# One MLP half step between the two parts of a head's first maximum, and the split of x behind the next head's roundings

## The chip, the cores and the metric

The kernel runs on one core of a Trainium2 chip. Its engines work side by side, each through its own instruction queue, in the order of that queue: TensorE (PE in the profile; its weight loads are PEld), VectorE (DVE), ScalarE (ACT), GpSimd (POOL) and SyncE (SP), which issues most of the DMAs. Where an instruction needs another engine's result, or a buffer that another engine still reads, it waits on a semaphore. The metric is the device time of one execution in microseconds (us), as the median of several runs. Every matmul writes a bank of PSUM; there are eight banks of 128 x 512 fp32, and ACT and DVE read them.

## The reference

Attention with a decay and a causal mask over 64 heads (8 batches of 8) of 576 positions and width 64, followed by an MLP without bias over all 4608 tokens.

```python
scores = scale * np.matmul(q, k.transpose(0, 1, 3, 2))
cum = np.cumsum(np.log(np.clip(f, 0.0001, 1.0)), axis=-1)
scores = np.where(causal, -1e9, scores + cum[:, :, :, None] - cum[:, :, None, :])
scores = scores - np.max(scores, axis=-1, keepdims=True)
attn = np.exp(scores)
attn = attn / (np.sum(attn, axis=-1, keepdims=True) + 1e-09)
x = np.matmul(attn, v)      # heads side by side: 4608 x 512
h = np.maximum(x @ w_in, 0.0)      # 512 -> 2048
out = h * h @ w_out      # 2048 -> 512
```

## The kernel before

**Slots.** The order of the program is written out by hand. A loop over slots n runs from before the first head to after the last. Head h has the six slots 6h to 6h+5, one for each unit u of its scores: a block of 128 keys against the queries that may see it (`UNITS`; the first one has 320 columns, the third 192). In slot n the loop (L810 on) emits, in this order: the split of the last slot's exponentials if it is still due (`split_last`), the score of unit u with its exponential (`score`), the products with V of the unit two slots back (`av_part`), steps that divide by the sums (`finish`), the events of the slot's first half, a share of the weight conversion (`cv`), MLP work (`fill(n, 0.5)`), the events of its second half, again `cv`, and `fill(n, 1.0)`. At the end `in_order` fixes that order on PE, ACT, DVE and POOL: no instruction passes another one of its engine.

**Maxima.** The maximum of each row of a head's scores is taken during the slots of the head before, in six units (`max_units`). A unit is a matmul of the rounded q (`r2`) by the rounded k (`kl0`) at L390, and a reduction by DVE at L398, which the profile shows as a custom operation and a read of the accumulator into the tile tcol. The first row block, that of the last 128 queries, has 576 columns, more than a bank holds. So it takes two units: maximum 0 with 256 columns, and maximum 1 with 320, whose reduction starts from the result of maximum 0. From head 10 on the events stand at `MAXIMA[1]`, slots 1.5, 2, 2.5, 3, 3.5 and 4 of the head before: maximum 0 in the second half of slot 6h+1, maximum 1 in the first half of slot 6h+2, maximum 2 in its second half. "Head 43's maximum 0" below means the one that is taken in head 43's slots (for head 44).

**Roundings.** `r2` and `kl0` are rounded copies of q and k. `prep` and, from head 20 on, `prep_split` make them on DVE (L335 and L336, or L357 and L358) in the second half of slot 6h, for the next head.

**MLP halves.** Chunks of 256 tokens (`T`), 16 steps each (`NF`). One step has two halves: `mlp1` (L605: 12 matmuls of 256 columns, x by w_in) and `mlp2` (L638: 6 matmuls of 512 columns, the squared relu by w_out), which belongs to the step before. `mlp_half` places them by turns. Each call first runs `bend` for the last `mlp1`, if that is still to come: ACT reads its bank for the relu (r, L620) and squares it (gh, L621), DVE makes the square and its low part (g, gl, L625 and L626). All `mlp1` write one bank, number 4 (`banks["h"]`), so each must wait until the relu of the one before has read it. With 12 and 6 matmuls per step and heads of 6 scores, one `mlp1` or `mlp2` stands between most groups of attention matmuls.

**Pace.** `fill` spreads a batch's halves evenly over the slots in which the next batch's attention runs. `ready[b]` is the slot from which the chunks that batch b completes are open: 53, 104, 152, 200, 248, 296, 344 and 392. Between two of them come 64 halves, or 96 (from slot 200 to 248, heads 33 to 41); `goal` is the count that is due at (n, part), and never above `limit`. After the loop, all that is left of the MLP follows in one run.

**Banks.** Scores and maxima share banks by turns (`banks["s"]`): four from the start of the MLP on, only two ([1, 2]) while chunk 1 is worked on (from head 10's last slot to head 17's slot 2), then four again.

**The split of x.** `split_x` makes of a chunk's x a rounded part xh (L590) and a low part xl (L591), both on DVE. It follows POOL's multiply of x by the reciprocals (`finish`, part 3, L537). For batches 1 to 7 it is an event of slot `ready[b] - 2`, that is slot 6h of head h = 17, 25, 33, 41, 49, 57 and 65 (the last behind the last head), in its first half; `finish` part 3 stands in the same slot, ahead of it.

Of the kernel before, what the change touches and what calls it, by code (L numbers as in the profile page):

```python
# [34 lines left out]
def decay_attention_relu2_kernel(  # L35
# [20 lines left out]
    NH, D, _, S = qk.shape  # L56
# [7 lines left out]
    T = 256  # L64
# [219 lines left out]
    NU = len(UNITS)  # L284
# [375 lines left out]
    def mlp_half(finished):  # L660
        bend()
        if halves[0] % 2:
            if len(steps) > 1:
                mlp2(*steps[-2])
        else:
            step = next_step()
            if step is None:
                return False
            c, fc = step
            if fc == 0:  # L670
                if c == 0:
                    banks.update(s=[1, 2, 3, 5], m=[], av=[0])
                if c == 1:
                    banks.update(s=[1, 2], o0=[3], o1=[5])
                if c == 2:
                    banks.update(s=[1, 2, 3, 5], o0=[6], o1=[7])
                split_x(c, finished)
            if fc > 0 and ("x", c + 1) not in mst and (c != 1 or ahead[0] == NF):
                split_x(c + 1, finished)
            mlp1(c, fc)  # L680
            ahead[c] += 1
            steps.append(step)
        halves[0] += 1
        return True
# [9 lines left out]
    MAXIMA = (0, 0.5, 1, 1.5, 2, 2.5), (1.5, 2, 2.5, 3, 3.5, 4)  # L694
# [7 lines left out]
    def split_last():  # L702
        while unsplit:
            split_p(*unsplit.pop())

    def fin(h, part):

        return (h + 1) * NU - 1 + DIVIDE[h >= H][part]
# [13 lines left out]
    ready = [fin(b * H + H - 1, 3) + 2 if b else H * NU + 5 for b in range(B)]  # L722

    def fill(n, part):

        b = sum(r <= n for r in ready)
        if b == 0:
            return
        r0 = ready[b - 1]
        r1 = ready[b] if b < B else r0 + H * NU  # L730
        limit, before = (2 * NF * (x * S // T) for x in (b, b - 1))
        goal = before + (limit - before) * (n - r0 + part) / (r1 - r0)
        if b == 1 and len(split_w) == NW:

            if not pace:
                pace.append((n + part, halves[0]))
            n0, h0 = pace[0]
            goal = h0 + (limit - h0) * (n + part - n0) / (r1 - n0)
        while halves[0] < min(goal, limit):
            split_last()  # L740
            if not mlp_half(b):
                break
# [11 lines left out]
    def at(n, half, do, *args):  # L754
        events.setdefault((n, half), []).append(lambda: do(*args))
# [22 lines left out]
        if not split:  # L778
            at((h - 1) * NU + (4 if h else 3), 0, turn_maxima, h)
    for b in range(B):  # L780
        at(ready[b] - (2 if b else 1), 0, split_x, b * S // T, b + 1)
    spun = psum.tile([P, 512], F32, name="bank6")

    def spin(n):
# [25 lines left out]
    for n in range(-2 * NU, last_slot + 1):  # L810
        live = 0 <= n < len(slots)
        split_last()
        if live:
            h, u = slots[n]
            score(h, u)
            if h >= NPLAIN:
                unsplit.append((h, u))
        for ha, ua in avs.get(n, ()):
            if ua < NU - 1:
                av_part(ha, ua, False)  # L820
            else:
                av_part(ha, ua, True)
                av_part(ha, ua - 1, True)
        for do, *args in fins.get(n, ()):
            do(*args)
        for do in events.get((n, 0), ()):
            do()
        wr = 0 if n < -NU // 2 else RATES[0 if n < 0 else 1 if n < ready[0] else 2]
        cv(wr / 2)
        fill(n, 0.5)  # L830
        for do in events.get((n, 1), ()):
            do()
        cv(wr / 2)
        fill(n, 1.0)
# [45 lines left out]
```

## Time and profile before

| what | us |
|---|---|
| median of 3 runs | 1202.7 (1198.0 to 1205.06) |
| the profiled execution's own time | 1200.4 |
| its span, first to last instruction | 1198.7 |

The mean clock granted to TensorE over the span is 0.995. The span has three parts: up to some 250 us, in which also the weights are converted and heads with other forms of the scores run; the heads from 18 to 63, about 16.2 us each (21.7 where a batch has 96 halves), up to some 1040 us; and the rest of the MLP alone. The work of each engine in one stretch of each part (us of the window, then busy us and, in brackets, instructions of PE, PEld, DVE, ACT and POOL; the granted clock; the share of time that DMA engines were busy, and GB/s):

```profile
100.00:200.00 100.00, 97.03 (x616) 80.46 (x614) 79.40 (x203) 64.11 (x158) 5.29 (x14) 1.00 0.45 119
700.00:800.00 100.00, 100.00 (x690) 91.93 (x689) 66.34 (x185) 63.37 (x165) 39.48 (x60) 1.00 0.20 48
1000.00:1100.00 100.00, 99.54 (x660) 90.53 (x659) 46.24 (x118) 44.35 (x114) 14.44 (x23) 1.00 0.08 22
```

A row of a timeline has the start in us from the span's begin, the duration in us, the engine, the line, the operation, output and inputs by the program's names, their shape, and a count. In square brackets stands how long the engine had been idle before it, and what released it. A matmul's row lasts longer than its share of PE, because matmuls overlap: the distance from one start to the next is what PE spends.

### The profile page before, as it was taken

To read this page: it belongs to the slowest core of one execution; us is meant where nothing else is said; L and a number is where in the kernel's file an instruction comes from. 1 tells how busy PE (TensorE), PEld (TensorE's weight loads), DVE (VectorE), ACT (ScalarE), POOL (GpSimd) and SP (SyncE) were. 2 spreads that over 40 slices of the span, in tenths; PEclk is the share of its full clock that TensorE was granted. 3 is DMA by queue.
4 is the path that set the end of the run, shared out by engine and by line. 5 is a ranking of instruction groups with operands and counts; after the bars stand their busy time and mean duration, and the time that the engine had idled before them with its cause. 6 is when DMAs were issued, how large, how long until landed. Compare 5 with 4: busy or idle time off the path is not lost. (4 is left out here: it accounts for less than half of the span.)

```text
span 1198.7 us, 23146 instructions
## 1 busy us (share of the span) xinstructions
PE 1174.7 (98%) x7770; PEld 1040.0 (87%) x7770; DVE 773.1 (64%) x2072; ACT 693.5 (58%) x1745; POOL 317.8 (27%) x510
## 2 busy tenths in 40 slices
PE   7999999999999999999999999999999999999998
PEld 4667887789998999899999899988999899999997
DVE  6888887666667666756666666676676766443232
ACT  4776666555666665665565656666665666533232
POOL 2110000123334343422222334344333434200000
PEclk8999999999999999999999999999999999999999
DMA  8885622221211121211111122112121112000000
GB/s 200 198 226 175 175 51 51 70 69 43 54 37 46 42 60 43 54 32 35 42 45 24 53 43 54 42 33 60 42 61 36 42 42 60 12 28 19 1 19 18
DMA packets 109778, 73.03 MB, mean 61 GB/s; under 512 B 90766, under 2 KB 90766, under 8 KB 109660
## 3 DMA queue, kind: packets, MB, share of 16 engines
q1 hardware_dynamic: 108936, 68.90, 22.6%
q0 software_dynamic: 720, 2.65, 1.0%
q8 instruction: 62, 1.02, 0.4%
q14 instruction: 56, 0.46, 0.1%
q10 hardware_dynamic: 4, 0.00, 0.0%
HBM read 58.41 MB, written 9.87 MB: 57 GB/s over the span
## 5 line engine op out<-in xcount | busy, mean ns | idle before, releaser
L638 PE MATMUL bank<-w,gh 128*128 128x512 f32 x1152 | 413.5, 399 | 0.0
L605 PE MATMUL bank<-xh,w 128*128 128x256 f32 x2304 | 331.5, 286 | 5.5 <-ACT r L620 5.4
L605 PEld LDWEIGHTS bank<-xh,w 128*128 128x128 f32 x2304 | 300.1, 189 | 16.9 <-ACT r L620 9.8
L470 DVE TENSOR_TENSOR pl<-p,ph 128x320 fp32r<-128x320 f32 (+4 forms) x288 | 175.4, 610 | 203.3 <-ACT ph L469 198.5
L638 PEld LDWEIGHTS bank<-w,gh 128*128 128x128 f32 x1152 | 217.5, 189 | 37.8
L638 PE MATMUL bank<-w,gl 128*128 128x512 f32 x576 | 227.0, 394 | 0.2 <-DVE gl L626 0.2
L469 ACT CAST ph<-p 128x320 fp32r<-128x320 f32 (+4 forms) x288 | 119.4, 415 | 162.8 <-POOL p L456 119.8
L456 POOL TENSOR_SCALAR_AFFINE_SELECT p<-p 128x128 f32<-128x128 f32 (+1 forms) x240 | 87.1, 363 | 392.1 <-ACT p L454 324.9
L620 ACT ACTIVATE r<-bank 128x256 f32<-128x256 f32 x288 | 109.7, 381 | 132.4 <-PE bank L605 118.3
L605 PE MATMUL bank<-xl,w 128*128 128x256 f32 x1152 | 184.6, 283 | 0.0
L454 ACT ACTIVATE p<-bank 128x320 f32<-128x320 f32 (+4 forms) x288 | 111.2, 386 | 117.9 <-PE bank L442 105.4
L625 DVE TENSOR_TENSOR g<-r 128x256 f32<-128x256 f32 x261 | 115.5, 443 | 94.3 <-ACT r L620 94.3
L626 DVE TENSOR_TENSOR gl<-g,gh 128x256 fp32r<-128x256 f32 x288 | 135.9, 472 | 47.9 <-ACT g L623 16.8
L398 DVE CUSTOM_DVE_ANT_0 bank<-bank,mz 128x256 f32<-128x256 f32 (+4 forms) x320 | 133.6, 432 | 49.7 <-PE bank L390 49.2
L605 PEld LDWEIGHTS bank<-xl,w 128*128 128x128 f32 x1152 | 158.4, 191 | 0.2 <-DVE xl L591 0.2
L621 ACT ACTIVATE gh<-r 128x256 fp32r<-128x256 f32 x288 | 120.4, 418 | 9.1
L390 PE MATMUL bank<-rk 66*128 66x320 f32 (+4 forms) x384 | 110.7, 318 | 12.3 <-DVE tcol L398 4.1
L638 PEld LDWEIGHTS bank<-w,gl 128*128 128x128 f32 x576 | 109.2, 190 | 15.1 <-DVE gl L626 1.7
L442 PE MATMUL bank<-rl 128*128 128x320 f32 x324 | 95.1, 294 | 0.0
L439 PE MATMUL bank<-rk 67*128 67x320 f32 x324 | 93.4, 288 | 0.1
L390 PEld LDWEIGHTS bank<-rk 66*128 66x128 f32 (+1 forms) x384 | 67.6, 182 | 28.7 <-DVE tcol L398 6.9
L480 PE MATMUL bank<-pl,vh 128*65 128x320 f32 (+4 forms) x336 | 91.3, 272 | 0.0
(103 smaller groups left out, 1485.3 us busy)
## 6 DMA issues: line engine op xcount, KB each, us to landing
qkraw<-in_qk SPq DMA_DIRECT2D x54, 288.0 KB
v<-in_v SPq DMA_DIRECT2D x64, 160.0 KB
out<-osb SPq DMA_DIRECT2D x36, 256.0 KB
den<-rdr SPq DMA_DIRECT2D x62, 144.0 KB
w<-in_w_in SPq DMA_DIRECT2D x16, 512.0 KB
w<-in_w_out SPq DMA_DIRECT2D x16, 512.0 KB
rk<-tcol SPq DMA_DIRECT2D x216, 0.5 KB
rl<-in_qk SPq DMA_DIRECT2D x10, 288.0 KB
```

What stands on the lines that cost most here:

```text
L390: nc.tensor.matmul(ps[:m, :n], st["r2"][:D + 2, q0:q0 + m], st["kl0"][:D + 2, k0:k0 + n], start=True, stop=True,)
L398: nc.vector.tensor_tensor_reduce(out=ps[:m, :n], in0=ps[:m, :n], in1=mz[:m, mo:mo + n], op0=ALU.add, op1=ALU.min, scale=-1.0, scalar=init, ...
L442: nc.tensor.matmul(ps[:kn, :n], st["l2"][:, k0:k0 + kn], st["r1"][:, q0:q1], start=False, stop=not added,)
L454: nc.scalar.activation(out=p[:kn, :n], in_=ps[:kn, :n], func=AF.Exp, scale=SCALE)
L469: nc.scalar.copy(out=ph[:kn, :n], in_=p[:kn, :n])
L470: nc.vector.tensor_tensor(out=pl[:kn, :n], in0=p[:kn, :n], in1=ph[:kn, :n].bitcast(F32), op=ALU.subtract,)
L605: nc.tensor.matmul(ph[:, :T], w[:, s, cc], x[:, cc, :], start=(cc == 0 and k == 0), stop=(cc == NCC - 1 and k == 2),)
L620: nc.scalar.activation(out=r, in_=ph[:, :T], func=AF.Relu)
L621: nc.scalar.activation(out=gh, in_=r, func=AF.Square)
L625: nc.vector.tensor_tensor(out=g, in0=r, in1=r, op=ALU.mult)
L626: nc.vector.tensor_tensor(out=gl, in0=g, in1=gh.bitcast(F32), op=ALU.subtract)
L638: nc.tensor.matmul(po, g[:, ts], w[:, s], start=(fc == 0 and k == 0), stop=(fc == NF - 1 and k == 2),)
```

## The change

Two edits; no instruction is added or left out, and only the order changes.

```diff
@@ fill(n, part)
             n0, h0 = pace[0]
             goal = h0 + (limit - h0) * (n + part - n0) / (r1 - n0)
+        if n % NU == int(MAXIMA[1][0]) and part == 1:
+            goal += 1
         while halves[0] < min(goal, limit):
             split_last()
             if not mlp_half(b):
@@
     for b in range(B):
-        at(ready[b] - (2 if b else 1), 0, split_x, b * S // T, b + 1)
+        at(ready[b] - (2 if b else 1), 1 if b else 0, split_x, b * S // T, b + 1)
```

The first edit raises the goal by one half step in the second `fill` of each slot 6h+1 (`int(1.5)` is 1), behind maximum 0 and ahead of the score of unit 2 and maximum 1. The goal of the next call is as it was, so the total doesn't change. It acts from slot 55 (head 9) on, and not where the goal has reached the batch's limit.

The second edit moves the split of x for batches 1 to 7 from the first half of slot `ready[b] - 2` to its second half. Events of one half run in the order in which they were entered, and those of the heads were entered first, so the split now comes after `prep` part 0 of the next head, which has the two roundings.

## The prediction

> **What bounds the kernel now.** I read the page first, then TensorE's waits, the chain that ended last, and the timelines around one head's first maximum.
>
> ```profile
> span 1198.7 us, 23146 instructions
> PE 1174.7 (98%) x7770; PEld 1040.0 (87%) x7770; DVE 773.1 (64%) x2072; ACT 693.5 (58%) x1745; POOL 317.8 (27%) x510
> L605 PE MATMUL bank<-xh,w 128*128 128x256 f32 x2304 | 331.5, 286 | 5.5 <-ACT r L620 5.4
> ```
>
> TensorE (PE) is busy for 98% of the span, and no other engine for more than 64%. So time is gained only where PE stands still, and each new stand of PE is lost unless it swallows an old one. The waits of PE alone (engine, line, what it waited for; us in total, times, longest):
>
> ```profile
> engine line waited for: us in total, times, longest us
> PE bank L605 <- ACT r L620: 5.4, 8, 0.8
> PE bank L390 <- DVE tcol L398: 4.1, 5, 1.0
> PE bank L390 <- DVE rk L358: 1.8, 3, 0.9
> PE bank L390 <- DVE rk L336: 0.8, 1, 0.8
> ```
>
> The change can win from two of these. Rows 2 to 4 are maxima (L390) that wait for a reduction on DVE (VectorE; tcol) or for the next head's roundings (rk): 6.7 us in all. Row 1 names the danger: the first product of an MLP step (mlp1, L605) waits for the relu (r, L620) on ACT (ScalarE), because all mlp1 share one PSUM bank, and the relu of the last mlp1 must have read it.
>
> **The change, first edit: where the half goes.** In `fill` the goal of a batch that does 64 halves in 48 slots is a whole number at the end of slot 6h+1, so there the kernel before places nothing. One more makes it place exactly one half, and the next call none. By parity that half is an mlp1. Per head PE's order was: mlp2, maximum 0, score of unit 2 with its value products, maximum 1, mlp1, maximum 2, mlp2. It becomes: mlp2, maximum 0, **mlp1**, score, value products, maximum 1, maximum 2, mlp2. The work is the same; mlp1 is only asked for earlier. ACT's order up to the relu doesn't change, since the relu is issued with the mlp2 ahead of maximum 0. Head 44, PE and ACT:
>
> ```profile
> 712.34 0.55 ACT L454 ACTIVATE p<-bank 128x448 f32<-128x448 f32 x1 [1.76 <-PE bank L442]
> ...
> 717.00 0.41 ACT L469 CAST ph<-p 128x256 fp32r<-128x256 f32 x1 [2.09 <-POOL rl L356]
> ...
> 722.13 0.38 ACT L620 ACTIVATE r<-bank 128x256 f32<-128x256 f32 x1
> ...
> 721.67 0.28 PE L390 MATMUL bank<-rk 66*128 66x256 f32 x1
> 721.79 0.25 PE L439 MATMUL bank<-rk 67*128 67x192 f32 x1
> ...
> 722.57 0.62 PE L605 MATMUL bank<-xh,w 128*128 128x256 f32 x3
> ```
>
> Maximum 0 starts at 721.67 and the score behind it at 721.79: there the moved mlp1 will stand. But the relu runs from 722.13 to 722.51, and mlp1 started 0.06 later, at 722.57. The old place had no slack at all. The new one asks 0.78 us sooner, so PE waits 722.57 − 721.79 = 0.78 us. The neighbour, head 43, has a little less:
>
> ```profile
> 705.71 0.25 PE L439 MATMUL bank<-rk 67*128 67x192 f32 x1
> ...
> 705.85 0.39 ACT L620 ACTIVATE r<-bank 128x256 f32<-128x256 f32 x1
> ...
> 706.49 1.11 PE L605 MATMUL bank<-xh,w 128*128 128x256 f32 x8
> ```
>
> Relu end 706.24, plus 0.06, less 705.71: 0.59 us. Here mlp1 started 0.25 us behind the relu, so it didn't wait before.
>
> Does the relu come earlier once PE stands? From 717.00 to the relu ACT has no idle time (none of its rows there shows any), on a run that begins behind POOL (GpSimd) and goes back to the exponential at 712.34, which waited 1.76 us for PE's score of unit 4. So it is with the exponentials at large:
>
> ```profile
> ACT p L454 <- PE bank L442: 105.4, 106, 1.8
> ```
>
> That score lies behind the new stand of the head before. So PE's delay moves the run along with it, and the stand comes back in each head.
>
> I read the same two times in each head concerned: 18 to 24, 26 to 32, 42 to 48, 50 to 56 and 58 to 63, 34 in all. (Heads 17, 25, 33, 41, 49 and 57 are at the batch's limit at that slot and get no extra half.) The first and the last:
>
> ```profile
> 252.36 0.38 ACT L620 ACTIVATE r<-bank 128x256 f32<-128x256 f32 x1
> 252.47 0.26 PE L439 MATMUL bank<-rk 67*128 67x192 f32 x1
> ...
> 1032.02 0.38 ACT L620 ACTIVATE r<-bank 128x256 f32<-128x256 f32 x1
> ...
> 1032.13 0.25 PE L439 MATMUL bank<-rk 67*128 67x192 f32 x1
> ```
>
> These two give 0.33 each, the others 0.52 to 0.86; the sum is **23.5 us**, a mean of 0.69.
>
> A stand also has a tail. Where PE waited for a relu, weights and matmul start together:
>
> ```profile
> 681.62 0.38 ACT L620 ACTIVATE r<-bank 128x256 f32<-128x256 f32 x1
> ...
> 682.05 1.01 PEld L605 LDWEIGHTS bank<-xh,w 128*128 128x128 f32 x8 [0.85 <-ACT r L620]
> 682.05 1.22 PE L605 MATMUL bank<-xh,w 128*128 128x256 f32 x8 [0.74 <-ACT r L620]
> ...
> 683.58 0.39 PE L638 MATMUL bank<-w,gh 128*128 128x512 f32 x1
> ...
> 1190.75 1.43 PE bank L605 x12
> ```
>
> From 682.05 to 683.58 is 1.53 us, against 1.43 for twelve undisturbed matmuls (the row of the chain): 0.10 for the weights that weren't loaded ahead. Heads like 44 pay this already, since their mlp1 starts on the relu's heels. I add it for the 16 that don't, like 43: 1.6 us. First term: 23.5 + 1.6 = **+25.1**. The Trainium skill ("TensorE: Matmul & The Clock Gate", the steps of what happens when a matmul is issued) says that PE pulls weight loads ahead of matmuls in flight, while matmuls keep their order. By that the 1.6 could go, and the 23.5 not; the load at 682.05, which waited with its matmul, doesn't agree for a load whose matmul is held, so I keep the 1.6.
>
> Heads 34 to 40 do 96 halves in 48 slots and have an mlp2 already between maximum 0 and the score; the moved mlp1 goes behind it (head 35):
>
> ```profile
> 540.16 0.40 PE L638 MATMUL bank<-w,gh 128*128 128x512 f32 x1
> ...
> 540.46 0.39 ACT L620 ACTIVATE r<-bank 128x256 f32<-128x256 f32 x1
> ...
> 541.56 0.25 PE L439 MATMUL bank<-rk 67*128 67x192 f32 x1
> ```
>
> The relu ends at 540.85, long before 541.56: no stand. Only in head 36 does it end about 0.1 us too late; with the tail 0.2 us. Without mlp2 as a cover, each would cost 0.75, like the others.
>
> **Heads 9 to 16** are the other kind: scores and maxima share two banks from head 10's end on, and maximum 1 waits until DVE has reduced maximum 0. Head 13:
>
> ```profile
> 162.49 0.25 PE L439 MATMUL bank<-rk 67*128 67x192 f32 x1
> ...
> 163.47 0.42 DVE L398 CUSTOM_DVE_ANT_0 bank<-bank,mz 128x256 f32<-128x256 f32 x1
> ...
> 164.00 0.42 PE L390 MATMUL bank<-rk 66*128 66x320 f32 x1 [0.54 <-DVE tcol L398]
> ```
>
> The 1.43 us of mlp1 between the two cover that wait. But maximum 2, and in heads 12 and 14 (no half in slot 6h+2 any more) the next score too, now follow maximum 1 at once on the same two banks, and wait for an exponential and for DVE's reduction. From both sides: the gain is at most the 4.1 us of the tcol row (less, since one of its five waits is head 17's); the cost is at most that row's mean, 0.8 us, in each of the six heads 11 to 16, so +5. The row nearest to both is the same one, so a head's new wait is worth about its old one, and about as many heads lose as win: I take **0**.
>
> **Second edit.** At slot 0 of heads 17, 25, ... DVE's queue held the split of x ahead of the next head's two roundings, and the split waits for POOL's multiply by the reciprocals. Head 25:
>
> ```profile
> 362.21 1.53 POOL L537 TENSOR_TENSOR xt<-xt,den 128x576 f32<-128x576 f32 x1 [1.55 <-DMA den<-rdr]
> ...
> 363.77 0.43 DVE L590 CAST xh<-xt 128x512 fp32r<-128x512 f32 x1 [1.32 <-POOL rl L356]
> ...
> 365.31 0.44 DVE L358 CAST rk<-qkraw 64x576 fp32r<-64x576 f32 x1
> 365.81 0.39 PE L390 MATMUL bank<-rk 66*128 66x256 f32 x1 [0.35 <-DVE rk L358]
> ```
>
> DVE idled 1.32 us ahead of L590; two roundings of about 0.45 fit in there. So maximum 0 no longer waits, and the split starts when it did. Nothing queued behind the split comes later: next is the low part of p (L470), now without two roundings ahead of it. Gained are the two rk rows, 1.8 + 0.8 = 2.6 us in heads 17, 25, 33 and 49, and four tails of 0.10: **−3.0**. At most it is −3.4, with tails of a whole weight load (0.19); at least −1.5, if half is taken back by the next wait, as in head 17, which still has two banks. POOL runs beside the roundings then, and here is a cost:
>
> ```profile
> 679.74 1.22 DVE L591 TENSOR_TENSOR xl<-xt,xh 128x1024 fp32r<-128x1024 f32 x1
> ...
> 679.85 1.27 POOL L456 TENSOR_SCALAR_AFFINE_SELECT p<-p 128x128 f32<-128x128 f32 x1 [0.83 <-ACT p L454]
> ...
> 700.64 0.29 POOL L456 TENSOR_SCALAR_AFFINE_SELECT p<-p 128x128 f32<-128x128 f32 x1
> ```
>
> A mask of 0.29 us took 1.27 beside a DVE instruction. If both roundings held the multiply up wholly, the split would start some 0.9 late, as late as before; only head 17's share, the 0.8 of its row, hangs on that. The Trainium skill ("GPSIMD Engine Reference", Key points) says POOL shares its SBUF interfaces with DVE. By it that share goes and the edit gives −2.2; these rows agree.
>
> **Sum**: 25.1 + 0.2 + 0 − 3.0 = **+22.3 us**. Made against the profiled execution, whose own time is 1200.4 (span 1198.7, 1.7 around it), that is 1222.7; the median of the three runs, 1202.7, lies 2.3 higher, so I forecast **1225**. Its own range goes from 1198 + 16 (23.5 without tails, −4.1 in heads 9 to 16, −3.4) to 1205 + 29 (25.3 + 5 − 1.5): 1214 to 1234.
>
> **Rivals.**
>
> ACT's run isn't tied to PE. POOL, whose work starts it, idles ahead of it with no releaser shown. If the run kept its own time, PE's first stand would leave the relu early in the next head, and the 23.5 would shrink to half (+9.5, so 1212) or to nothing (1200). Against it speaks the row of the exponentials, 105.4 us of ACT waiting for PE's scores. Chance 0.11, 1199 to 1213.
>
> Faster: in the 34 heads the relu ends before the moved mlp1 asks, because the queues ahead of it run differently, and the half only covers what it was put over. This decides from a relu 0.3 to 0.9 us earlier. Then the tcol and rk waits go: −4.1 − 3.0, so 1202.7 − 7.1 = 1196. For it: 6.7 us of such waits are there. Against it: ACT had no gap to give. Chance 0.06, 1190 to 1197.
>
> The change does nothing of note, the goal being passed already: the order of PE in heads 18 to 63 (nothing between maximum 0 and the score) speaks against it. About 1200; chance 0.02.
>
> Worse: maxima 1 and 2 now come back to back, and DVE reduces them ahead of the low part of unit 2. If that made another stand of 0.3 in each of 41 heads, 12 more: 1237. Against it: four banks there, and the tcol row counts only five waits in all, none of them where there are four. Chance 0.06, 1234 to 1246.
>
> Forecast 0.75. The range 1207 to 1236 leaves out most of the second and third rival, half of the first and half of the last, about 0.17. Faster by over 0.5% (6 us, about what a measurement can tell from no change): 0.06; within it: 0.08; slower: 0.86.
>
> **What would show it.** Right: TensorE's waits get a row L605 <- ACT r of some 20 us over about 40 times; head periods of the 64-half batches grow by 0.6 to 0.9 and those of heads 34 to 40 don't; the rk waits at L390 are gone; the tail after head 63 is the same length. Wrong: the relu row stays at 5.4, or ACT's idle time ahead of it grows instead.

## The result and the profile after

| kernel | median, us | runs | ratio to before (95% interval) |
|---|---|---|---|
| before | 1201.2 | 4 | |
| changed | 1229.6 (1228.0 to 1232.6) | 4 | 1.0247 (1.021 to 1.0285) |

The change makes the kernel 28.3 us slower; 22.3 were forecast. The profiled execution of the changed kernel took 1228.0 us. From its page, the span, the engines' totals and the group of mlp1's first eight matmuls:

```profile
span 1226.3 us, 23090 instructions
PE 1180.5 (96%) x7770; PEld 1038.6 (85%) x7770; DVE 780.8 (64%) x2072; ACT 696.7 (57%) x1745; POOL 311.2 (25%) x510
L605 PE MATMUL bank<-xh,w 128*128 128x256 f32 x2304 | 333.3, 287 | 24.2 <-ACT r L620 24.2
```

The matmuls are the same and PE's busy time hardly differs; what grew is the idle time ahead of L605, from 5.5 to 24.2 us. TensorE's waits of the changed kernel, the largest:

```profile
engine line waited for: us in total, times, longest us
PE bank L605 <- ACT r L620: 24.2, 45, 1.0
PE bank L480 <- DVE pl L470: 4.1, 3, 1.8
PE bank L638 <- DVE gl L626: 1.9, 2, 1.0
PE bank L390 <- DVE tcol L398: 1.8, 2, 1.0
...
PE bank L480 <- ACT rl L362: 1.2, 1, 1.2
```

Three things are to be seen here. The relu row rose by 18.8 us, over 45 waits instead of 8. The rk rows are gone, and tcol fell from 4.1 to 1.8: both edits did cover the waits they stand over. And rows are there that the forecast didn't have: the value products (L480) wait for the low part of p (pl), and an mlp2 (L638) waits for gl, 1.9 us where the kernel before had 0.2. Head 44 of the changed kernel on the timeline, PE and ACT:

```profile
734.00 0.28 PE L390 MATMUL bank<-rk 66*128 66x256 f32 x1
734.90 1.21 PE L605 MATMUL bank<-xh,w 128*128 128x256 f32 x8 [0.62 <-ACT r L620]
...
734.46 0.38 ACT L620 ACTIVATE r<-bank 128x256 f32<-128x256 f32 x1
```

Maximum 0 starts at 734.00 and what follows could start 0.12 later; mlp1 starts at 734.90, 0.06 behind the relu. The stand is 0.78 us, as worked out from the trace of before. (The row's 0.62 counts from the modelled end of maximum 0.)

Where the time went can be read per head. From the timelines of both kernels I took the start of each head's first score and compared what each stretch took, in us against the profiled execution of before. The same was done for every experiment, so that one table serves them all:

| kernel | up to head 9 | 9 to 16 | 17 | the 34 heads with a moved mlp1, and the end | 34 to 40 | 25, 33, 41, 49, 57 | sum |
|---|---|---|---|---|---|---|---|
| changed | −3.4 | +4.2 | −1.6 | +24.1 | −0.1 | +4.4 | +27.6 |
| only_half | −3.4 | +2.3 | −1.8 | +24.2 | −0.1 | −1.6 | +19.4 |
| only_split | +3.2 | −0.3 | −1.5 | −0.1 | 0 | +5.8 | +7.0 |
| two_banks_before | +5.6 | +0.3 | −2.0 | +14.4 | 0 | +0.6 | +18.8 |
| two_banks_after | +5.8 | +3.0 | −2.1 | +14.5 | −0.1 | +1.8 | +22.9 |
| relu_first_after | +7.5 | +2.7 | −1.7 | +10.4 | −0.1 | +2.0 | +20.6 |
| half_early_heads | 0 | +3.2 | −1.8 | 0 | 0 | −0.5 | +1.0 |
| split_later | +4.9 | −0.3 | 0 | +0.7 | 0 | −1.5 | +3.9 |
| split_pool_later | −0.3 | 0 | −1.4 | 0 | 0 | −1.4 | −3.1 |
| half_three_heads | −3.2 | −1.6 | −1.6 | +0.1 | 0 | +1.9 | −4.5 |
| relu_first_before | +3.2 | +0.8 | −0.7 | −2.3 | 0 | −5.0 | −3.8 |
| all_three | +0.1 | −2.6 | −0.8 | −2.1 | 0 | −6.6 | −11.7 |

The first column holds no edit of anybody: up to head 9 all these programs place the same work. It differs by 11 us because of the clock (last section), and so does much of the column of head 17. The medians average over that. How far a column can be trusted is seen where a kernel changes nothing in its heads. The columns of the 34 heads and of heads 34 to 40 then show 0.1 at most, that of heads 9 to 16 up to 0.8. The column of the five heads is the weakest: half_three_heads shows +1.9 there (1.7 of it a clock step) and only_half −1.6, though neither has an edit in them.

### The profile page after: what moved, and what is told of

Read it like the earlier page. It is cut to its first block, busy times and chain, and to the rows that moved or that the text cites. A ratio compares the mean times of both kernels' runs of the same rounds, so it can differ in the third digit from the quotient of the medians.

```text
span 1226.3 us, 23090 instructions
## 1 busy us (share of the span) xinstructions
PE 1180.5 (96%) x7770; PEld 1038.6 (85%) x7770; DVE 780.8 (64%) x2072; ACT 696.7 (57%) x1745; POOL 311.2 (25%) x510
## 3 DMA queue, kind: packets, MB, share of 16 engines
q1 hardware_dynamic: 108936, 68.90, 22.3%
q8 instruction: 62, 1.02, 0.4%
## 5 line engine op out<-in xcount | busy, mean ns | idle before, releaser
L638 PE MATMUL bank<-w,gh 128*128 128x512 f32 x1152 | 414.3, 400 | 0.0
L605 PE MATMUL bank<-xh,w 128*128 128x256 f32 x2304 | 333.3, 287 | 24.2 <-ACT r L620 24.2
L605 PEld LDWEIGHTS bank<-xh,w 128*128 128x128 f32 x2304 | 299.3, 189 | 45.6 <-ACT r L620 39.0
L470 DVE TENSOR_TENSOR pl<-p,ph 128x320 fp32r<-128x320 f32 (+4 forms) x288 | 180.1, 626 | 203.0 <-ACT ph L469 200.5
L638 PEld LDWEIGHTS bank<-w,gh 128*128 128x128 f32 x1152 | 217.6, 189 | 38.2
L638 PE MATMUL bank<-w,gl 128*128 128x512 f32 x576 | 227.6, 395 | 1.9 <-DVE gl L626 1.9
L456 POOL TENSOR_SCALAR_AFFINE_SELECT p<-p 128x128 f32<-128x128 f32 (+1 forms) x240 | 82.8, 345 | 439.0 <-ACT p L454 388.2
L605 PE MATMUL bank<-xl,w 128*128 128x256 f32 x1152 | 184.7, 283 | 0.0
L625 DVE TENSOR_TENSOR g<-r 128x256 f32<-128x256 f32 x261 | 124.2, 476 | 93.8 <-ACT r L620 93.8
L626 DVE TENSOR_TENSOR gl<-g,gh 128x256 fp32r<-128x256 f32 x288 | 132.8, 461 | 49.1 <-ACT g L623 17.7
L605 PEld LDWEIGHTS bank<-xl,w 128*128 128x128 f32 x1152 | 158.4, 191 | 0.2 <-DVE xl L591 0.2
L638 PEld LDWEIGHTS bank<-w,gl 128*128 128x128 f32 x576 | 109.3, 190 | 17.1 <-DVE gl L626 3.5
L390 PE MATMUL bank<-rk 66*128 66x320 f32 (+4 forms) x384 | 102.0, 314 | 5.5 <-DVE tcol L398 1.8
L480 PE MATMUL bank<-pl,vh 128*65 128x320 f32 (+4 forms) x336 | 91.2, 272 | 5.4 <-DVE pl L470 4.1
L481 PE MATMUL bank<-ph,v 128*64 128x320 f32 (+4 forms) x336 | 91.2, 271 | 0.0
```

Source lines behind the costliest of these rows:

```text
L390: nc.tensor.matmul(ps[:m, :n], st["r2"][:D + 2, q0:q0 + m], st["kl0"][:D + 2, k0:k0 + n], start=True, stop=True,)
L470: nc.vector.tensor_tensor(out=pl[:kn, :n], in0=p[:kn, :n], in1=ph[:kn, :n].bitcast(F32), op=ALU.subtract,)
L605: nc.tensor.matmul(ph[:, :T], w[:, s, cc], x[:, cc, :], start=(cc == 0 and k == 0), stop=(cc == NCC - 1 and k == 2),)
L625: nc.vector.tensor_tensor(out=g, in0=r, in1=r, op=ALU.mult)
L626: nc.vector.tensor_tensor(out=gl, in0=g, in1=gh.bitcast(F32), op=ALU.subtract)
L638: nc.tensor.matmul(po, g[:, ts], w[:, s], start=(fc == 0 and k == 0), stop=(fc == NF - 1 and k == 2),)
```

## The experiments

The theory after the result: the moved mlp1 stands behind the relu, because all mlp1 share one bank; and the second edit doesn't gain, but costs. The rivals: that the order itself (two maxima back to back, DVE's queue) makes the stands, and that the second edit gains what was forecast.

**Each edit alone.** *only_half* keeps the goal's line and puts the split back; *only_split* is the other way round.

> First edit alone, the split of x where it was before. Theory (the moved mlp1 stands behind the relu of the one shared bank, and the second edit as a whole costs some 2.8 us): about 1227; the row L605 <- ACT r stays at 24 us, the rk waits at L390 (2.6 us) come back, the waits of the value products (L480) for pl go. Rival (the second edit gains its 3 us and the half costs more than it seems): about 1232.

> Second edit alone. Theory (DVE's queue is full at that place, so putting the split behind the roundings only moves PE's stand from maximum 0 to the value product that waits for pl): no rk wait at L390, but 4 to 6 us of L480 <- DVE pl in heads 17, 25, 33 and 49; about 1203, within 0.5% of before. Rival (as predicted, DVE had idle time there): no wait for pl, about 1198.

Measured: only_half 1224.8 us, ratio 1.0181 (1.0154 to 1.0207); only_split 1206.8, ratio 1.0039 (1.0019 to 1.006). In only_half the 34 heads cost 24.2 us, as with both edits, and TensorE's first wait is

```profile
PE bank L605 <- ACT r L620: 24.3, 45, 1.0
```

So the first edit alone makes this row. The second edit, meant as a gain, costs about 0.4%. Its waits are (TensorE's, only_split):

```profile
PE bank L480 <- DVE pl L470: 5.8, 4, 1.9
...
PE bank L480 <- ACT rl L362: 1.2, 1, 1.2
```

The rk rows have gone and 7.0 us of waits for pl have come. (The second row names L362, which ended last, but it is a wait for pl as well: in head 33 the low part ends at 500.30 and L480 starts at 500.44, and in head 25, whose row names pl, 368.42 and 368.57.) In head 41 comes a wait of 0.93 for gl.

**The relu and the bank.** Two kernels give mlp1 two banks from chunk 2 on. PSUM has no bank free, so one is taken from the scores and maxima; the control does the same to the kernel before.

```diff
                 if c == 2:
-                    banks.update(s=[1, 2, 3, 5], o0=[6], o1=[7])
+                    banks.update(s=[1, 2, 3], h=[4, 5], o0=[6], o1=[7])
```

> The changed kernel, but from chunk 2 on mlp1 turns over two PSUM banks and scores and maxima over three instead of four. Theory (the cost is the relu of one shared bank): L605 <- ACT r falls from 24 us to under 3, heads 18 to 63 take the time that they took before, about 1206. Rival (the order itself costs, by maxima back to back or DVE's queue): the 24 us stay or turn into waits at L390 and L439, above 1218.

> Control: the same banks in the kernel before. Theory: only the 4 us that mlp1 waited for the relu from chunk 2 on can go, so about 1198 if three banks for scores and maxima are enough; rival (three are too few): slower than 1203 with new waits at L390 and L439.

Measured: two_banks_after 1218.6 us, ratio 1.0124 (1.0093 to 1.0154); two_banks_before 1216.0, ratio 1.0121 (1.0092 to 1.0151). TensorE's waits in the control, then in the changed kernel with two banks:

```profile
PE bank L390 <- DVE tcol L398: 12.8, 31, 1.0
...
PE bank L605 <- ACT r L620: 0.7, 1, 0.7
```

```profile
PE bank L390 <- DVE tcol L398: 10.5, 35, 1.0
...
PE bank L605 <- ACT r L620: 2.4, 4, 1.0
```

Both totals missed what the theory gave, since three banks are too few for scores and maxima: they now wait for tcol, about 30 times, and the 34 heads take 14.4 us longer in the control. (The row counts only idle time behind the modelled end of a matmul. By the starts, the time from mlp1 to maximum 2 and from there to the next matmul is 14.3 us longer in 33 of these heads.) But between the two kernels the 34 heads differ by 14.5 − 14.4 = 0.1 us, where with one bank the same edit costs them 24.1. With the shared bank taken away the cost of moving mlp1 is gone. Nor does the moved mlp1 pay for itself here by covering tcol: in these heads PE idles 7.5 us ahead of L390 in the control and 7.4 with the edit, and the row's fall of 2.3 us lies in other heads.

**The relu's place in ACT's queue.** In the changed kernel, the relu and the square of slot 6h+1 go ahead of the cast of p.

```diff
         while halves[0] < min(goal, limit):
+            if n % NU == 1 and part == 0.5 and n > ready[1]:
+                bend()
             split_last()
```

> The changed kernel, but in slot 6h+1 of heads 17 on, relu and square of the last mlp1 are issued ahead of the cast of p (0.46 us on ACT) instead of behind it. Theory (PE's stand is the end of the relu less PE's arrival): the relu ends 0.46 sooner, the stands of 0.78 and 0.59 become about 0.32 and 0.13, L605 <- ACT r falls from 24 to about 9, about 1214. Rival (something else holds the moved mlp1, or what is made to wait takes the gain): within 4 us of 1229.

Measured: 1217.3 us, ratio 1.0132 (1.0098 to 1.0165), 12.2 us less than the changed kernel; the 34 heads cost 10.4 instead of 24.1. Waits of TensorE, and head 44 (PE's maximum 0 and mlp1, ACT's relu) in this kernel:

```profile
PE bank L605 <- ACT r L620: 7.6, 19, 1.0
```

```profile
736.61 0.38 ACT L620 ACTIVATE r<-bank 128x256 f32<-128x256 f32 x1
736.62 0.28 PE L390 MATMUL bank<-rk 66*128 66x256 f32 x1
...
737.04 1.22 PE L605 MATMUL bank<-xh,w 128*128 128x256 f32 x8
```

The relu now starts with maximum 0, not 0.46 behind it, and mlp1 waits only from 736.74 to 737.04, 0.30 us. In head 44 the stand shrinks by as much as the relu comes earlier, and PE's order is that of the changed kernel. In the other heads mlp1 starts 0.05 us behind the relu as well; head 18's stand, 0.32 in the changed kernel, is gone.

**Heads 9 to 16.** *half_early_heads* has the first edit in these heads alone (`and n < ready[1]`), *half_three_heads* in heads 13, 15 and 16. There the moved half stands alone between maximum 0 and the next score; in heads 10, 12 and 14 two halves come to stand there, and none between the next two maxima and the score behind them:

```diff
+        if n // NU in (13, 15, 16) and n % NU == 1 and part == 1:
+            goal += 1
```

> First edit in heads 9 to 16 alone, nothing else. Theory (there the covered waits for tcol are paid back by relu, gl and the banks of maxima back to back): about 4 us slower than before, 1205, and heads 18 to 63 take what they took before. Rival (prediction: gain and loss even out): 1201.

> The kernel before, with the extra half in heads 13, 15 and 16 alone. Theory (there the moved half is the only one beside maximum 0 and its relu or gl is long done, so the wait for tcol is covered and nothing takes its place): heads 13, 15 and 16 shorter by 0.6, 1.0 and 0.6, in all 2.2 us, nothing else changed; about 1199. Rival (the gain is given back in the heads behind): heads 9 to 17 together as long as before.

Measured: 1203.6 us, ratio 1.0018 (0.9998 to 1.0038), and 1199.6 us, ratio 0.9991 (0.9973 to 1.0008). Neither total can be told from no change, but the heads can. In half_early_heads heads 13, 15 and 16 are shorter by 0.64, 1.01 and 0.60, and heads 10, 11, 12 and 14 longer by 0.67, 2.31, 0.90 and 1.61. In half_three_heads the three gains are the same (0.65, 1.02, 0.61) and 10, 12 and 14 are as before; head 11, which has no edit in it, is 0.68 longer, within its scatter (0.81 in relu_first_before, which leaves it alone too). Heads 11 and 14 of the changed kernel show what the gain was paid with (PE):

```profile
128.66 0.50 PE L638 MATMUL bank<-w,gl 128*128 128x512 f32 x1 [0.95 <-DVE gl L626]
```

```profile
180.71 1.21 PE L605 MATMUL bank<-xh,w 128*128 128x256 f32 x8 [0.97 <-ACT r L620]
...
184.07 0.25 PE L439 MATMUL bank<-rk 67*66 67x64 f32 x1 [0.51 <-DVE tcol L398]
```

In head 11 the moved half is an mlp2, and its second operand gl isn't there yet. In head 14 the relu is behind two ACT steps of the weight conversion, and then the score follows two maxima on two banks.

**The split of x.** *split_later* moves it a whole slot in the kernel before, so that the low part of p of unit 0 is ahead of it too. *split_pool_later* has the second edit, and POOL's subtraction of the next head one slot later.

```diff
-        at(ready[b] - (2 if b else 1), 0, split_x, b * S // T, b + 1)
+        at(ready[b] - 1, 0, split_x, b * S // T, b + 1)
```

```diff
+                late = part == 2 and h % H == 2 and h > NPLAIN + 4
-                at((h - 1) * NU + SPLIT[part], 1, prep, h, part)
+                at((h - 1) * NU + SPLIT[part] + late, 1, prep, h, part)
```

> The kernel before, with the split of x moved one whole slot (first half of slot 6h+1 instead of 6h), so that the roundings and also the low part of p of unit 0 are ahead of it. Theory (PE needs both before it needs the split): neither rk waits at L390 nor pl waits at L480, about 1198. Rival (POOL's subtraction, which the roundings release, slows pl on DVE wherever the split stands): waits for pl of 2 to 4 us stay, about 1201.

> Second edit alone, and POOL's subtraction for k (L365) of heads 26, 34, 42, 50 and 58 one slot later, so that it doesn't run beside pl. If the collision makes the stand: pl takes 0.9 instead of 2.1 us for two, the waits of L480 in heads 25, 33 and 49 fall to 0.3 or less. If the length of DVE's queue makes it: they stay at 0.9 or more. Total 1198 to 1202.

Measured: 1201.1 us, ratio 0.9999 (0.998 to 1.0018), and 1199.9 us, ratio 0.9991 (0.997 to 1.0013). In the five heads both are 7 us shorter than only_split (−1.5 and −1.4 against +5.8, of which 1.7 is a clock step), but neither total is lower than before. First head 25 of only_split (POOL, DVE, PE):

```profile
366.21 1.86 POOL L365 TENSOR_TENSOR rl<-qkraw,rk 64x576 fp32r<-64x576 f32 x1
366.73 2.09 DVE L470 TENSOR_TENSOR pl<-p,ph 128x320 fp32r<-128x320 f32 x2
...
368.57 0.33 PE L480 MATMUL bank<-pl,vh 128*65 128x320 f32 x1 [1.48 <-DVE pl L470]
```

Then the same place in split_pool_later:

```profile
361.04 1.72 DVE L358 CAST rk<-qkraw 64x576 fp32r<-64x576 f32 x1
...
363.73 0.89 DVE L470 TENSOR_TENSOR pl<-p,ph 128x320 fp32r<-128x320 f32 x2
...
365.81 1.43 POOL L365 TENSOR_TENSOR rl<-qkraw,rk 64x576 fp32r<-64x576 f32 x1
```

Beside POOL's subtraction the two instructions for pl take 2.09 us, alone 0.89; and the subtraction 1.86 instead of 1.43. Earlier roundings had released it earlier, into the low parts that PE waits for. In the kernel before it had fallen on DVE's g, which no wait of PE names there:

```profile
365.68 0.88 DVE L470 TENSOR_TENSOR pl<-p,ph 128x320 fp32r<-128x320 f32 x2
365.84 2.00 POOL L365 TENSOR_TENSOR rl<-qkraw,rk 64x576 fp32r<-64x576 f32 x1 [0.76 <-DVE rk L358]
366.48 1.63 DVE L625 TENSOR_TENSOR g<-r 128x256 f32<-128x256 f32 x1
```

The subtraction's row overlaps that of pl here too, and pl isn't slowed; so overlap alone doesn't say which DVE instruction pays. A rounding is slowed as well, 1.72 us at 361.04 in split_pool_later, beside POOL's multiply. In split_later the collision is still there, but it falls on the split (L591), and the first pl has been done:

```profile
368.74 0.71 DVE L470 TENSOR_TENSOR pl<-p,ph 128x320 fp32r<-128x320 f32 x1 [0.94 <-ACT ph L469]
...
369.91 1.81 DVE L591 TENSOR_TENSOR xl<-xt,xh 128x512 fp32r<-128x512 f32 x1
```

The waits for rk and pl are gone in split_later; what it wins is lost again elsewhere, in head 17, whose wait for tcol is 2.29 us instead of 0.95, and behind head 63, where mlp1 waits 0.5 for the late split. In split_pool_later, with the subtraction out of the way, L480 still waits 0.27 in head 25, none in head 33 and 0.68 in head 49, where 0.3 or less was expected. So it is both: what stands ahead of pl in DVE's queue, and what POOL does beside it. In head 17, where the next head has no such subtraction on POOL, the second edit leaves a stand of some 0.9 for pl in the place of some 0.8 for rk: there only the queue counts, and nothing is won.

**What beats both.** A late relu makes mlp1 wait in the kernel before too, in slot 6h+5 of seven heads (the eighth wait, in head 9, has another cause): the relu, in slot 6h+4, follows a cast that waits for POOL's mask. *relu_first_before* puts it ahead of that cast.

```diff
         while halves[0] < min(goal, limit):
+            if n % NU == 4 and part == 0.5 and n > ready[1]:
+                bend()
             split_last()
```

> The kernel before; from slot 105 on, in slot 6h+4 the relu and square of the last mlp1 are issued ahead of the cast of p, which waits there for POOL's mask. Theory (the same relu makes the 8 waits of L605 that were there before): the row L605 <- ACT r falls from 5.4 us to about 1, total lower by 4: about 1197. Rival (the cast, now later, holds up the value products or the next relu): no gain, new waits at L480 or L605 in other slots.

Measured: 1192.7 us, ratio 0.9927 (0.9902 to 0.9953). The waits of L605 that it aimed at are gone:

```profile
PE bank L605 <- ACT r L620: 0.7, 1, 0.7
```

Head 41 of it, ACT and PE:

```profile
680.35 0.38 ACT L620 ACTIVATE r<-bank 128x256 f32<-128x256 f32 x1
...
681.89 0.57 ACT L469 CAST ph<-p 128x448 fp32r<-128x448 f32 x1 [0.71 <-POOL p L456]
...
681.88 1.20 PE L605 MATMUL bank<-xh,w 128*128 128x256 f32 x8
```

The relu is done 1.15 us before mlp1 asks for its bank, and the cast, still waiting for the mask, holds up nobody on PE. The gain is larger than expected (7.2 us by the heads from 18 on, 4 expected). A part of it may be scatter: the row of waits for rk (L358), which the edit doesn't aim at, fell from 1.8 to 0.9 us. The rest stays open.

*all_three* joins this to the half in heads 13, 15 and 16 and to the second edit with POOL's subtraction put off.

> The extra half in heads 13, 15 and 16 alone, the second edit with POOL's subtraction one slot later, and the relu ahead of the cast in slot 6h+4. Theory (three separate stands of PE): -2.2, -1.4 and -4, about 1194, 0.6% faster than before. Rival (DVE or POOL are then the next to be late): not under 1198.

Measured: 1188.9 us, ratio 0.9899 (0.9874 to 0.9924), faster than both kernels and 5 us below what was expected. Most of the gain is that of relu_first_before: the two intervals overlap, so the totals don't show what the other two parts add. Its page:

```profile
span 1187.0 us, 23219 instructions
PE 1170.7 (99%) x7770; PEld 1039.6 (88%) x7770; DVE 771.4 (65%) x2072; ACT 702.5 (59%) x1745; POOL 307.2 (26%) x510
```

## Why the prediction held, step by step

**The stand of the moved mlp1: right, in place and size.** 25.1 us were forecast for the 34 heads, 24.1 were measured. It holds term by term: in the 33 heads from 18 to 62, the same two times in the kernel before give stands of 23.2 us and the changed kernel has 22.7; its twelve matmuls of mlp1 take 1.5 us longer in all, where 1.6 were put down for the tail. The run of ACT does move along with PE: heads 18 and 63, for which the same stand was read, are 0.41 and 0.39 us longer. The rival that ACT's run isn't tied to PE is out, and so is the one of maxima back to back: with two banks for mlp1 the same order costs nothing.

**Heads 34 to 40: right.** 0.2 forecast, −0.1 measured; the mlp2 ahead covers the relu.

**Heads 9 to 16: the mechanisms right, the size off.** Forecast 0, measured between +2.3 and +4.2, of which in the changed kernel 1.6 are a clock step in head 14. The failing step is "a head's new wait is worth about its old one, and about as many heads lose as win". Three heads win 2.2 together, four lose 4.6 to 5.5. The waits for an exponential and for DVE's reduction were named there; that a moved mlp2 would wait for gl, and a moved mlp1 for a relu behind the weight conversion, was not.

**The second edit: wrong, in sign too.** Forecast −3.0; measured +5.8 in the five heads of only_split and +4.4 in the changed kernel (with one clock step of 1.7 in head 49 in each), and +2.0 in relu_first_after, which has the edit too, beside its own, and no clock step there. The size is uncertain by some 2 us; no kernel shows the gain. The step that failed is "Nothing queued behind the split comes later: next is the low part of p (L470), now without two roundings ahead of it". It took DVE's instructions at the durations they had in the trace of before. But the roundings also release POOL's subtraction, and where the two engines overlap one of them can be slowed. The forecast did weigh that, with the mask of 0.29 us that took 1.27, but let POOL's multiply alone pay for it. In head 25 of only_split the multiply took 1.48 us, in the kernel before 1.53; the first rounding beside it took 1.72. And the forecast left out what else POOL would then start earlier. The Trainium skill ("GPSIMD Engine Reference", Key points) says the two share their SBUF interfaces; these runs agree, with 0.89 against 2.09 us for the same two DVE instructions.

**The sum.** 22.3 forecast, 28.3 measured by the medians. Against the forecast, the heads give −1.0 for the stands, −0.3 for heads 34 to 40, +2.6 to +4.2 for heads 9 to 16 and +6 to +7 for the second edit (without and with its clock step). That adds up to 7 to 10 more, where the medians show 6 more; the medians' own uncertainty is about 4 us. So the forecast came near because its largest term was right; the two smaller terms that were wrong both missed to the same side.

## What to carry to other kernels

When PE is the bound and buffers are shared by turns, moving a matmul earlier is free only while its buffer's last reader is done by then; the reader's end and the earliest start of the moved work stand in the trace of the kernel before, and their difference is the price. A wait that is covered in one head can be paid in forty. And an instruction that is released sooner releases others: ask what those run beside, on engines that slow each other, and whether the one they hit is the next that the bound waits for.

## What the runs showed of the hardware that was not expected

**Short stands can be followed by 3.4 us at half the clock.** In all these traces the clock granted to PE is either 1.0 or 0.5, and the spells at 0.5 last 3.4 us or multiples of it. They come not only behind long idle times. Head 49 of the changed kernel, two windows (us of the window; busy us and instructions of PE, PEld, DVE, ACT and POOL; clock; DMA):

```profile
817.00:821.00 4.00, 2.15 (x13) 1.74 (x12) 3.97 (x7) 3.16 (x9) 2.56 (x3) 1.00 0.01 1
821.00:825.00 4.00, 4.00 (x19) 3.82 (x18) 2.53 (x10) 1.15 (x3) 0.35 (x1) 0.57 0.04 4
```

One stand of 1.85 us (for pl) was followed by a window in which the clock was 0.57 in the mean, and PE issued 19 matmuls where the next 4 us had 30. The stand and the spell, which loses half of 3.4 us, so cost about 3.6 together. In the kernel before, two stands of 0.77 and 0.95 us in head 17 were followed by the same:

```profile
232.00:235.00 3.00, 1.68 (x9) 1.31 (x10) 2.90 (x9) 0.84 (x3) 0.29 (x1) 0.97 0.45 102
235.00:237.00 2.00, 2.00 (x11) 2.00 (x11) 0.72 (x3) 0.00 (x0) 0.00 (x0) 0.50 0.04 0
```

It doesn't happen each time. relu_first_after has the same stand of 1.85 us in head 49, and two_banks_before stands of 0.78 and 0.95 in head 17, and the clock stayed at 1.0 in both. What decides isn't shown. Where there was only one stand of 0.6 to 0.9 us per head, no spell followed in any of the traces.

**The start decides most of the scatter between the profiled executions.** Up to 90 us the mean clock was 1.00 in the changed kernel's profile and 0.87 in that of relu_first_after, though the two programs are the same up to there:

```profile
0.00:90.00 90.00, 82.39 (x484) 55.32 (x485) 71.53 (x218) 61.56 (x145) 16.75 (x48) 1.00 0.82 208
```

```profile
0.00:90.00 90.00, 82.76 (x400) 54.01 (x401) 63.88 (x195) 55.81 (x130) 16.39 (x46) 0.87 0.78 193
```

Between the two, head 9 starts 10.9 us apart (−3.4 and +7.5 in the table), which 0.13 of 90 us, 11.7, accounts for. Over all thirteen profiles the time lost to the clock up to head 9 goes from 0 to 12 us, and the start of head 9 follows it. A single run of this kernel therefore can't show a gain of 5 us; the starts of the heads can, as far as their own scatter allows.
